# Spreading one more half of the attention weights by DMA, and loading the first weight matrix from two queues

## The chip, the cores and the metric

The kernel runs on one core of one Trainium2 chip. The metric is the device time of one execution in microseconds (us). PE is the TensorE matmul engine, PEld its weight loads, DVE the vector engine, ACT the scalar engine, POOL GpSimd, SP the engine that here only issues DMA. "The trace" is one profiled execution of a kernel; a kernel's timed set is 4 to 11 executions.

## The reference

One transformer block in bf16, 2048 positions of 1024 features: layer norm, a dilated local attention (32 heads, 8 keys for each query), the output projection, then a gated MLP whose gate mixes all positions. What matters here is the attention:

```python
qkv = (layernorm(x) @ wqkv)                 # wqkv: 1024 x 3072, wq is its first third
idx = pos[:, None] - 2 * arange(8)[None]    # 8 keys, two apart
logits = einsum('bhsd,bhswd->bhsw', q, k[idx]) * scale   # masked where idx < 0
attn = softmax(logits, axis=-1)
o = einsum('bhsw,bhswd->bhsd', attn, v[idx])
h = x + o @ wo                              # then the MLP block on layernorm(h)
```

## The kernel before

The positions are worked on in four chunks of 512. Before the main loop the kernel loads the first x tiles (128 positions each) and the weights wq in eight pieces of 256 KB, one for each group of 128 input features:

```python
dma(xts[0][0:64, :], x2d[0:64, :])            # dma = the SP queue
A.dma_start(xts[0][64:P, :], x2d[64:P, :])    # A.dma_start = the ACT queue
x_slot(1)
A.dma_start(xts[1], x2d[P:2 * P, :])
wsb = [wtile([P, KT, D], "wq", "wA"), ...]
for kt in range(KT):                          # KT = 8
    if kt == 6:
        load_x(2)
    dma(wsb[0][:, kt, :], wq_view[:, kt, 0:D])
load_x(3)
dma(wsb[1][:], wq_view[:, :, D:2 * D])        # wk, one DMA of 2 MB
```

Chunk 0's query projection consumes them at once. An x tile is normalized on DVE (`ln`), transposed on PE (`xpose`), and the transposes of tile i + 1 stand inside the matmuls of tile i, ahead of piece 5 (`QSPLIT = 5`):

```python
for i in range(TPC):                          # 4 tiles
    acc = new_acc()
    for kt in range(KT):
        if kt == 2 and i == 0:
            xpose(0, xns[0], (5, KT)); ln(1)
        if kt == QSPLIT and i + 1 < TPC:
            xpose(i + 1, xns[i + 1], (0, 4), (4, KT))
        for nh in range(2):
            T.matmul(acc[:, nh, :], xnT[0][:, kt, i * P:(i + 1) * P], wsb[0][:, kt, nh * CH:(nh + 1) * CH], ...)
    if i + 2 < TPC:
        ln(i + 2)
    ...
```

From then on all work is put into a static order for each engine by a small list scheduler in the kernel (`add(engine, cost, function, dependencies, ...)`).

After the softmax a weight exists once for each head and has to be spread over that head's 4 partitions before DVE can multiply it with v. For chunks 1 to 3 this is done by DMA (`ABDMA`): store the weights to DRAM from the ACT queue, load them back from the POOL queue with each row read four times. For chunk 0 it is done on PE, by matmuls with a 0/1 matrix `B4`, in two halves of four matmuls. Each matmul uses 32 of the 128 rows of the array, and the result is copied out of PSUM (the memory that matmuls write to) by ACT or DVE:

```python
ABDMA = (0, 1, 1, 1)
...
wait = add("DMA", BSLACK if hw else 0.0, lambda: None, [prev])
for sh in range(2):
    def pbm(sh=sh, ws=ws, hw=hw):
        if sh == 0:
            pb = ps_att.tile([P, 2, 4, P], FP32, name="pb", tag="L")      # one slot
        else:
            pb = ps_acc.tile([P, 2, 4, P], FP32, name="pba", tag="acc")
        for j in range(2):
            sq = 2 * sh + j
            T.matmul(pb[:, j], B4[32 * sq:32 * sq + 32, :], st["attn"][32 * sq:32 * sq + 32, ws, :],
                     start=True, stop=True, tile_position=(32 * sq, 0))
    ...
    eng = "DVE" if (hw == 0 and sh == 1) else "ACT"
    # a copy of pb into AB[:, hw, ...] on that engine
```

## Time and profile before

| | before |
|---|---|
| time, median of 4 | 725.91 us (725.59 to 726.45) |
| span of the profiled run | 723.9 us |
| PE busy | 718.5 us, 99% |
| DVE, ACT busy | 57%, 33% |
| matmuls | 3458 |

Two lines of the page: busy time of each engine with its share of the span and its count of instructions, and the chain of waits by engine.

```profile
PE 718.5 (99%) x3458; PEld 364.4 (50%) x3458; DVE 413.0 (57%) x435; ACT 240.0 (33%) x304; POOL 48.6 (7%) x56
...
PE 98%; DMA 1%; ACTq 0%; DVE 0%; SPq 0%; issue 0%
```

The second line is the chain of waits: followed back from the last instruction, 98% of the span is PE behind PE. Only PE work that goes away, idle time of PE that closes, or a new wait of PE can change the time. The idle time is all at the start. The timeline of PE (start, length, engine, line, what, how many; in brackets an idle stretch just before and what ended it):

```profile
7.45 1.04 PE L308 MATMUL acc<-wq,xnT 128*128 128x512 bf16 x4 [0.16 <-ACT xnT L269]
8.33 0.33 PE L267 MATMUL tpa<-csb,xn 128*128 128x128 bf16 x3
8.50 1.67 PE L308 MATMUL acc<-wq,xnT 128*128 128x512 bf16 x6
10.28 0.62 PE L267 MATMUL tpa<-csb,xn 128*128 128x128 bf16 x8
10.74 0.59 PE L308 MATMUL acc<-wq,xnT 128*128 128x512 bf16 x2
11.58 3.44 PE L308 MATMUL acc<-wq,xnT 128*128 128x512 bf16 x14 [0.25 <-DMA wq<-in_A_wqkv_dram]
14.86 0.61 PE L267 MATMUL tpa<-csb,xn 128*128 128x128 bf16 x8
```

L308 is the query projection, L267 the transposes of an x tile: tile 1's at 10.28, tile 2's at 14.86. Matmuls in a row cost 0.216 us each, so ten of them (2.16 us) with three small transposes should not need the 2.83 us from 7.45 to 10.28. There are holes here, and more up to 12.27, where wq piece 7 comes. From tile 2's transposes on, PE is dense.

Here is the broadcast on PE, in the same timeline. L553 are the broadcast matmuls, L396 ordinary projections:

```profile
67.21 1.05 PE L491 MATMUL L<-part,csb 128*32 128x512 bf16 x16
68.19 7.99 PE L396 MATMUL acc<-xnT,wk 128*128 128x512 bf16 x36
76.11 0.39 PE L553 MATMUL pb<-attn,csb 32*128 32x512 bf16 x2
76.12 0.39 PE L553 MATMUL pba<-attn,csb 32*128 32x512 bf16 x2
76.44 1.09 PE L396 MATMUL acc<-xnT,wk 128*128 128x512 bf16 x4
77.46 0.39 PE L553 MATMUL pba<-attn,csb 32*128 32x512 bf16 x2
77.61 0.39 PE L553 MATMUL pb<-attn,csb 32*128 32x512 bf16 x2
77.93 3.67 PE L396 MATMUL acc<-xnT,wk 128*128 128x512 bf16 x16
81.44 1.89 PE L396 MATMUL acc<-xnT,wv 128*128 128x512 bf16 x8
```

There are two breaks into the projection, one for each half.

### The profile page before, as it was taken

How to read it: one execution, taken by the hardware profiler on the slowest of the kernel's cores; microseconds unless marked ns; L12 is line 12 of the kernel's file. 1: busy time of each engine (PE TensorE's matmuls, PEld its weight loads, DVE VectorE, ACT ScalarE, POOL GpSimd, SP SyncE). 2: the span in 40 equal slices, each digit the busy share in tenths (PEclk: the TensorE clock that was granted, in tenths of full speed). 3: DMA queues.
4: the chain of work that ended last, by engine and by line, in shares of the span. 5: the costliest groups of instructions: out<-in, count | busy, mean ns of one | idle time of the engine just before them, and what ended most of it. 6: DMA issues, size and time to landing. Idle time of an engine off the chain costs nothing.

```text
span 723.9 us, 8455 instructions
## 1 busy us (share of the span) xinstructions
PE 718.5 (99%) x3458; PEld 364.4 (50%) x3458; DVE 413.0 (57%) x435; ACT 240.0 (33%) x304; POOL 48.6 (7%) x56
## 2 busy tenths in 40 slices
PE   8999999999999999999999999999999999999998
PEld 3666665666644444445445444444444444444444
DVE  5698999989998999876970202222222222222222
ACT  4389552633346785776735520000000000000000
POOL 0011200111002102000113000000000000000000
PEclk9999999999999999999999999999999999999999
DMA  8996464567664832642339979453116311120001
GB/s 303 278 299 134 145 175 148 159 213 254 211 255 147 230 149 75 229 138 71 140 113 261 251 196 293 158 139 120 33 43 138 119 35 44 39 87 7 1 22 66
DMA packets 119166, 107.09 MB, mean 148 GB/s; under 512 B 72568, under 2 KB 97304, under 8 KB 119128
## 3 DMA queue, kind: packets, MB, share of 16 engines
q1 hardware_dynamic: 110496, 73.88, 35.1%
q0 software_dynamic: 7616, 31.50, 12.7%
q10 hardware_dynamic: 1016, 1.18, 0.5%
q8 instruction: 27, 0.44, 0.3%
q14 instruction: 11, 0.09, 0.0%
HBM read 58.24 MB, written 31.52 MB: 124 GB/s over the span
## 4 chain that ended last, share of the span: by engine, by line
PE 98%; DMA 1%; ACTq 0%; DVE 0%; SPq 0%; issue 0%
PE acc L869 27%; PE acc L396 21%; PE acc L762 13%; PE acc L712 13%; PE acc L891 13%; PE acc L647 8%; PE acc L308 2%; DMA xp<-in_A_x_dram 1%; DMA wq<-in_A_wqkv_dram 1%; PE L L491 1%; PE tpa L267 0%; ACTq L227 0%; PE pb L553 0%; DVE ot L893 0%; SPq L234 0%; PE pba L553 0%
## 5 line engine op out<-in xcount | busy, mean ns | idle before, releaser
L452 DVE TENSOR_TENSOR prod<-qT,kT 128x4096 bf16<-128x4096 bf16 (+1 forms) x36 | 73.1, 2049 | 3.4 <-ACT kT L402 3.4
L712 PEld LDWEIGHTS <-hnT 128*128 128x128 bf16 x512 | 50.1, 98 | 47.2
L891 PEld LDWEIGHTS <-zg 128*128 128x128 bf16 x462 | 45.2, 98 | 51.8
L590 DVE TENSOR_TENSOR prod<-vT,AB 128x4096 bf16<-128x4096 bf16 (+1 forms) x31 | 64.2, 2083 | 0.8
L592 DVE TENSOR_TENSOR oT<-oT,prod 128x4096 bf16<-128x4096 bf16 (+1 forms) x31 | 64.4, 2079 | 0.1
L893 DVE TENSOR_TENSOR ot<-acc,hr 128x1024 bf16<-128x1024 f32 (+2 forms) x18 | 19.9, 1106 | 73.1 <-PE acc L891 73.1
L891 PE MATMUL acc<-wout_a,zg 128*128 128x512 bf16 (+1 forms) x264 | 58.2, 373 | 0.0
L712 PE MATMUL acc<-win_1467,hnT 128*128 128x512 bf16 x256 | 58.0, 379 | 0.0
L396 PE MATMUL acc<-xnT,wk 128*128 128x512 bf16 x256 | 56.7, 380 | 0.0
L762 PE MATMUL acc<-hnT,win_1667 128*128 128x512 bf16 x256 | 56.2, 379 | 0.0
L396 PE MATMUL acc<-xnT,wv 128*128 128x512 bf16 x256 | 55.9, 379 | 0.0
L647 PE MATMUL acc<-wo_sb,oT 128*128 128x512 bf16 x256 | 55.9, 379 | 0.0
L407 ACT CAST stg<-acc 128x1024 bf16<-128x1024 f32 x36 | 36.4, 1010 | 55.6 <-PE acc L396 48.3
L396 PEld LDWEIGHTS <-wk 128*128 128x128 bf16 x256 | 36.7, 145 | 18.8 <-issue 0.9
L396 PEld LDWEIGHTS <-wv 128*128 128x128 bf16 x256 | 37.0, 145 | 18.2
L891 PE MATMUL acc<-wout_b,zg 128*128 128x512 bf16 (+1 forms) x198 | 44.4, 373 | 0.0
L712 PE MATMUL acc<-win_1562,hnT 128*128 128x512 bf16 (+1 forms) x256 | 44.2, 326 | 0.0
L762 PE MATMUL acc<-hnT,win_1673 128*128 128x512 bf16 x192 | 42.4, 379 | 0.0
L396 PE MATMUL acc<-xnT,wq 128*128 128x512 bf16 x192 | 42.1, 379 | 0.0
L719 ACT ACTIVATE u<-acc 128x1024 bf16<-128x1024 f32 (+1 forms) x32 | 29.4, 918 | 35.1 <-PE acc L712 35.1
L647 PEld LDWEIGHTS <-oT 128*128 128x128 bf16 x256 | 25.1, 98 | 30.1
L762 PEld LDWEIGHTS <-win_1667 128*128 128x128 bf16 x256 | 25.0, 98 | 29.9 <-issue 0.4
(271 smaller groups left out, 955.1 us busy)
## 6 DMA issues: line engine op xcount, KB each, us to landing
z_d<-z1s SPq DMA_DIRECT2D x28, 256.0 KB, 2.6
z1c<-z_d SPq DMA_DIRECT2D x28, 256.0 KB, 2.7
z_d<-u SPq DMA_DIRECT2D x12, 448.0 KB, 2.5
xr<-in_A_x_dram SPq DMA_DIRECT2D x16, 256.0 KB, 2.9
h_d<-hb SPq DMA_DIRECT2D x16, 256.0 KB, 2.0
hr<-h_d SPq DMA_DIRECT2D x16, 256.0 KB, 3.2
out_dram<-ot SPq DMA_DIRECT2D x15, 256.0 KB, 2.0
xp<-in_A_x_dram SPq DMA_DIRECT2D x14, 256.0 KB, 5.6
```

The costliest lines, as they stand in the source:

```text
L396: G["mmins", c, xi, dp] = T.matmul(G[key][:, j, :], wv[:, kt, dl, :], xnT[c][:, kt, :], start=(kt == 0), stop=(kt == KT - 1))
L407: A.copy(stg[:], G[key][:])
L452: V.tensor_tensor(qs[w]["prod"][:, d0:d1], qT[:, d0:d1], kT[:, d0:d1, o:o + CH], op=ALU.mult)
L590: V.tensor_tensor(dst[:, :, sq].rearrange("p d (q s) -> p d q s", q=nq), vv, abb, op=ALU.mult)
L592: V.tensor_tensor(oTs[c][:, :, sq], oTs[c][:, :, sq], pvs[w, q0][:, :, sq], op=ALU.add)
L647: T.matmul(st["acc", il][:, nh, :], oTs[c][:, dl, il * P:(il + 1) * P], wo_sb[:, dl, nh * CH:(nh + 1) * CH], start=(dl == 0), stop=(dl == ...
L712: T.matmul(accf[:, n0:n1], hnTs[c][:, il, kt, :], wins[hf][:, kt, n0:n1], start=(kt == 0), stop=(kt == KT - 1))
L719: A.activation(st["u", il][:, hf * 1024:hf * 1024 + wd], G["accz", c, il, hf][:].rearrange("p a b -> p (a b)")[:, 0:wd], ACTF.Gelu_apprx_t ...
L762: T.matmul(G["accy", c, fp][:, j, :].rearrange("p (a b) -> p a b", a=TPC), wt[:, kt, f0 * P:(f0 + 1) * P], hnTs[c][:, :, kt, :], start=(kt ...
L869: m_ = T.matmul(acc[:, j, :], z2sb[a][:, f * P:(f + 1) * P], wspT[:, a, :], start=(a == 0), stop=(a == NT - 1))
L891: T.matmul(acc[:, m0 - n0:m1 - n0], zg[:, f, il * P:(il + 1) * P], wt[:, f0, m0:m1], start=(f == 0), stop=(f == NF - 1))
L893: V.tensor_tensor(ot[:, n0:n1], acc[:, 0:n1 - n0], hr[:, n0:n1], op=ALU.add)
```

## The change

The intent: take the second half of chunk 0's broadcast off PE (its consumer comes late enough for the DMA's latency), and get wq into the core sooner by loading pieces from both queues, with the x tiles that are needed later behind them.

```diff
-BSLACK = 1.0
-ABDMA = (0, 1, 1, 1)
+ABDMA = ((1,), (0, 1), (0, 1), (0, 1))
@@
-    A.dma_start(xts[1], x2d[P:2 * P, :])
     wsb = [wtile([P, KT, D], "wq", "wA"), wtile([P, KT, D], "wk", "wA"), wtile([P, KT, D], "wv", "wB")]
-    for kt in range(KT):
-        if kt == 6:
-            load_x(2)
-        dma(wsb[0][:, kt, :], wq_view[:, kt, 0:D])
+    for q, kt in ((dma, 0), (A.dma_start, 1), (dma, 2), (A.dma_start, None), (dma, 4), (A.dma_start, 3), (dma, 5), (dma, 6), (dma, 7)):
+        if kt is None:
+            q(xts[1], x2d[P:2 * P, :])
+        else:
+            q(wsb[0][:, kt, :], wq_view[:, kt, 0:D])
+    load_x(2)
     load_x(3)
@@ attention(c), for each half hw
-            if ABDMA[c]:
+            if by_dma:                       # by_dma = hw in ABDMA[c]
+                def keep(...):  A.dma_start(attn_d[c][hw]..., st["attn"][:, ws, :]...)
+                def spread(...): dma_w(st["AB"][:, hw]..., attn_d[c][hw]....to_broadcast([H, 4, 2048]))
+                kept = add("ACT", 0.35, keep, [prev], prio=0.0)
+                abs_[hw, 0] = abs_[hw, 1] = add("DMA", 6.5, spread, [kept], take=None if hw else "part")
                 continue
-            wait = add("DMA", BSLACK if hw else 0.0, lambda: None, [prev])
  ... (the matmul branch stays for the first half; the old all-or-nothing DMA branch goes)
```

More of the change, by code (lines that the diff above doesn't have):

```diff
@@ L531, in attention, with new_ab, at, keep @@
         prev = add("DVE", 0.92, rec, [prev], prio=3.0)
-        abs_, ats = {}, []
+        abs_ = {}
+        def new_ab():
+            st["AB"] = att.tile([P, 2, TPC, W_WIN // 2, P], BF16, name="AB", tag="part", bufs=2)
         for hw in range(2):
             ws = slice(4 * hw, 4 * hw + 4)
-            def at(ws=ws, hw=hw):
-                if hw == 0 and not ABDMA[c]:
-                    st["AB"] = att.tile([P, 2, TPC, W_WIN // 2, P], BF16, name="AB", tag="part", bufs=2)
+            by_dma = hw in ABDMA[c]
+            def at(ws=ws, alloc=not hw and not by_dma):
+                if alloc:
+                    new_ab()
                 V.tensor_tensor(st["attn"][:, ws, :], st["sme"][:, 1, ws, :], st["rinv"][:].unsqueeze(1).to_broadcast([P, 4, P]), op=ALU.mult)
-            prev = add("DVE", 0.61, at, [prev], prio=3.0, lat=0.1, take="part" if hw == 0 and not ABDMA[c] else None, free="prod" if hw else None)
-            ats.append(prev)
-            if ABDMA[c]:
+            prev = add("DVE", 0.61, at, [prev], prio=3.0, lat=0.1, take=None if hw or by_dma else "part", free="prod" if hw else None)
+            if by_dma:
+                def keep(hw=hw, ws=ws):
+                    A.dma_start(attn_d[c][hw].rearrange("h q w s -> q h (w s)"), st["attn"][:, ws, :].rearrange("p w s -> p (w s)"))
+                def spread(hw=hw):
+                    if hw == 0:
+                        new_ab()
+                    dma_w(st["AB"][:, hw].rearrange("p q w s -> p (q w s)"),
+                          attn_d[c][hw].rearrange("h q w s -> h (q w s)").unsqueeze(1).to_broadcast([H, 4, 2048]))
+                kept = add("ACT", 0.35, keep, [prev], prio=0.0)
+                abs_[hw, 0] = abs_[hw, 1] = add("DMA", 6.5, spread, [kept], take=None if hw else "part")
                 continue
-            wait = add("DMA", BSLACK if hw else 0.0, lambda: None, [prev])
             for sh in range(2):
@@ L554, in pbm, with cp @@
                                  start=True, stop=True, tile_position=(32 * sq, 0))
-                pm = add("PE", 0.2, pbm, [wait], prio=1.0, take="acc" if sh else "L", lat=0.2)
-                eng = "DVE" if (hw == 0 and sh == 1) else "ACT"
-                def cp(sh=sh, ws=ws, hw=hw, eng=eng):
-                    (V.tensor_copy if eng == "DVE" else A.copy)(
-                        st["AB"][:, hw, 2 * sh:2 * sh + 2], st["pb", hw, sh][:])
-                abs_[hw, sh] = add(eng, 1.25 if eng == "DVE" else 0.91, cp, [pm], prio=1.0 if eng == "ACT" else 2.9,
-                                   free="acc" if sh else "L", lat=0.15)
-        if ABDMA[c]:
-            for k in range(2):
-                def keep(k=k):
-                    A.dma_start(attn_d[c][k].rearrange("h q w s -> q h (w s)"), st["attn"][:, 4 * k:4 * k + 4, :].rearrange("p w s -> p (w s)"))
-                def spread(k=k):
-                    if k == 0:
-                        st["AB"] = att.tile([P, 2, TPC, W_WIN // 2, P], BF16, name="AB", tag="part", bufs=2)
-                    dma_w(st["AB"][:, k].rearrange("p q w s -> p (q w s)"),
-                          attn_d[c][k].rearrange("h q w s -> h (q w s)").unsqueeze(1).to_broadcast([H, 4, 2048]))
-                kept = add("ACT", 0.35, keep, [ats[k]], prio=0.0)
-                abs_[k, 0] = abs_[k, 1] = dma_op(6.5, spread, [kept])
-            abs_[0, 0].take = ("part",)
+                pm = add("PE", 0.2, pbm, [prev], prio=1.0, take="acc" if sh else "L", lat=0.2)
+                eng = "DVE" if sh else "ACT"
+                def cp(sh=sh, hw=hw, eng=eng):
+                    (V.tensor_copy if eng == "DVE" else A.copy)(st["AB"][:, hw, 2 * sh:2 * sh + 2], st["pb", hw, sh][:])
+                abs_[hw, sh] = add(eng, 1.25 if sh else 0.91, cp, [pm], prio=2.9 if sh else 1.0, free="acc" if sh else "L", lat=0.15)
         G["at", c] = prev
```

## The prediction

> **What bounds the kernel now.** PE. The page has PE busy 718.5 of 723.9 us, and the chain of waits is 98% PE: after 12.27 us every step of it up to 720.5 us is a matmul behind a matmul, granted clock 1.00 throughout. So only two things can move the time: PE work that goes away, and the bubbles before 12.27 us. DVE (57%) and ACT (33%) are off the chain.
>
> **Spread of chunk 0's second half.** Removed: four of the eight broadcast matmuls (32x512), two copies of ACT (1.02 us each) out of PSUM, one accumulator slot. Added: one store of the weights (issue on ACT about 0.5 to 1.1 us) and one broadcast load of 512 KB from POOL, as chunks 1 to 3 already do. In the chain the stretch 76.18 to 78.00 us holds the eight broadcast matmuls and four ordinary ones; ordinary ones cost 0.216 us in the chain (64 in 13.81 us), so the eight cost 1.82 - 0.86 = 0.96 us and four about 0.48 us. All of that is on PE, so all of it is gained: -0.48 us. The new path: weights ready 75.4, store about 3 us, load 4.7 us median to landing: about 84.5 us. The timeline's first multiply that needs it (window step 4) starts at 92.2; the output projection that waits for the last of these starts at 114.4 and DVE is done at 110.3. So nothing there should wait; ACT's relief (about 1.5 us) is worth nothing.
>
> **Start.** PE lost between 7.45 and 12.27 us, in the fine timeline: 0.35 us for wq piece 4, 0.3 for x tile 1's normalized tile (10.28), 0.4 for piece 6 (11.58), 0.25 for piece 7 (12.27). The DMA view says that engines are busy 0.9 to 1.05 from 4 to 11 us and pieces land 0.68 us apart: it is bandwidth, not issue. The Trainium skill, "DMA: Bandwidth & Descriptors", section "Issuing engines are not separate DMA queues", says that several issuing engines share the same 16 DMA engines and save issue time only; this trace agrees (300 GB/s while both queues carry data, 390 to 410 afterwards with one).
> So a second queue gives no bandwidth. It changes order: x tiles 2 and 3 move behind wq. The last wq piece should land about 0.65 us earlier (256 KB less before it, near 11.6 us), but x tile 2 lands near 12.2 in place of 10.88, and x tile 1, now behind a wq piece on its queue, near 8.2 in place of 7.56. From landing to a normalized tile takes 2.7 us: tile 1's transposes near 10.9 (10.28 before), tile 2's near 14.9 (14.86 before). Bubbles for wq turn into bubbles for x; from there PE is dense. Start: about 0, between -0.6 and +0.8 us.
>
> **Prediction.** 725.87 - 0.48 - 0.1: 725.3 us, range 724.5 to 726.2. Faster by over 2%: 0.01; within 2%: 0.98; slower: 0.01.
>
> **What would show it.** PE matmuls 3454 instead of 3458; only one pair of copies out of the broadcast's PSUM tiles; the chain near 76 us shorter by 0.5 us; the spread's load landing before 90 us with no DVE wait on it. At the start: piece 7 no longer last to be waited for; DVE's wait for x tile 2 longer; tile 2's transposes within 0.6 us of 14.86. After that the chain again all PE.
>
> **What would make it wrong.** The ACT queue getting less than half of the packets, so that x tile 1 or wq piece 3 lands past 9.5 us (+1 us or more); a faster ramp of two queues, which would give up to -0.7; ACT's table load pushed behind its DMA issues past 5.6 us; the list order of the later work changing so that PE waits somewhere, which nothing in the trace prepares.

## The result

| | before | after |
|---|---|---|
| time, median of 4 | 725.91 us (725.59 to 726.45) | 725.23 us (724.50 to 725.79) |
| span of the profiled run | 723.9 us | 723.8 us |
| first query matmul | 7.45 us | 7.16 us |
| transposes of x tile 1 | 10.28 us | 11.52 us |
| transposes of x tile 2 | 14.86 us | 15.43 us |
| last addition of DVE | 720.55 us | 720.50 us |
| from tile 2's transposes to that addition ("the body") | 705.69 us | 705.07 us |

The ratio is 0.9989, with a 95% interval from 0.9972 to 1.0007: the same within the noise of the set. The measured 725.23 lies 0.07 from the predicted 725.3.

The table's last rows split the profiled run in two. The body became 0.62 us shorter, the start 0.57 us longer, and in this pair of traces the sum is about nothing (the timed medians differ by 0.68 us). The same two lines of the page after:

```profile
PE 714.0 (99%) x3392; PEld 364.1 (50%) x3454; DVE 413.0 (57%) x435; ACT 238.2 (33%) x302; POOL 49.6 (7%) x57
...
PE 98%; DMA 1%; issue 0%; DVE 0%; ACTq 0%; ACT 0%
```

PE's count is not a fall of 66: 62 matmul records are missing from this trace, and the weight loads, one for each matmul, give 3454, four fewer than before. ACT has two copies fewer. PE's start, where the two waits are now piece 3 of wq (9.86) and tile 1's normalized x (11.52):

```profile
7.16 1.04 PE L308 MATMUL acc<-wq,xnT 128*128 128x512 bf16 x4
8.03 0.33 PE L267 MATMUL tpa<-csb,xn 128*128 128x128 bf16 x3
8.20 0.59 PE L308 MATMUL acc<-wq,xnT 128*128 128x512 bf16 x2
9.86 1.02 PE L308 MATMUL acc<-wq,xnT 128*128 128x512 bf16 x4 [1.07 <-DMA wq<-in_A_wqkv_dram]
11.52 0.62 PE L267 MATMUL tpa<-csb,xn 128*128 128x128 bf16 x8 [0.63 <-DVE xn L255]
11.97 3.62 PE L308 MATMUL acc<-wq,xnT 128*128 128x512 bf16 x15
15.43 0.61 PE L267 MATMUL tpa<-csb,xn 128*128 128x128 bf16 x8
```

Behind 11.52 PE is dense: 11.97 + 16 x 0.216 = 15.43, so tile 2, which now comes last, was not waited for. DVE's timeline shows when the tiles came (L243 is the first instruction on an x tile). Here are tile 1 and tile 2, before:

```profile
7.59 0.69 DVE L243 BATCH_NORM_STATS2 bnst<-xp 128x6 f32<-128x512 bf16 x1 [0.52 <-DMA xp<-in_A_x_dram]
...
10.90 0.69 DVE L243 BATCH_NORM_STATS2 bnst<-xp 128x6 f32<-128x512 bf16 x1 [0.68 <-DMA xp<-in_A_x_dram]
```

and after:

```profile
8.82 0.69 DVE L243 BATCH_NORM_STATS2 bnst<-xp 128x6 f32<-128x512 bf16 x1 [1.90 <-DMA xp<-in_A_x_dram]
...
12.18 0.69 DVE L243 BATCH_NORM_STATS2 bnst<-xp 128x6 f32<-128x512 bf16 x1 [0.71 <-DMA xp<-in_A_x_dram]
```

Tile 1 is 1.23 us later, behind piece 1 on the ACT queue. That it comes later repeats in the experiments below, the size does not: DVE began on tile 1 at 8.08 to 8.82 us in the four traces with the split queues (after, e2, e4, e11), and at 6.80 to 7.96 in the seven with the old start. The broadcast after, with one break instead of two:

```profile
67.78 1.05 PE L491 MATMUL L<-part,csb 128*32 128x512 bf16 x16
68.76 7.13 PE L396 MATMUL acc<-xnT,wk 128*128 128x512 bf16 x31
75.83 0.39 PE L563 MATMUL pb<-attn,csb 32*128 32x512 bf16 x2
75.83 0.39 PE L563 MATMUL pba<-attn,csb 32*128 32x512 bf16 x2
76.15 5.40 PE L396 MATMUL acc<-xnT,wk 128*128 128x512 bf16 x24
81.39 1.89 PE L396 MATMUL acc<-xnT,wv 128*128 128x512 bf16 x8
```

(One of the 32 ordinary matmuls of the second line has lost its record.) From L491 to the first matmul of wv it takes 13.61 us, 14.23 before: the 0.62 us of the body are all here. The new path is not waited for: POOL issues the load at 79.93, it lands at 83.61, and DVE's first multiply with that half starts at 92.39, straight behind its previous work.

### The profile page after: what moved, and what is told of

It is laid out like the page before. It is cut to its first block, busy times and chain, and to the rows that moved or that the text cites. A ratio compares the mean times of both kernels' runs of the same rounds, so it can differ in the third digit from the quotient of the medians.

```text
span 723.8 us, 8387 instructions
## 1 busy us (share of the span) xinstructions
PE 714.0 (99%) x3392; PEld 364.1 (50%) x3454; DVE 413.0 (57%) x435; ACT 238.2 (33%) x302; POOL 49.6 (7%) x57
## 4 chain that ended last, share of the span: by engine, by line
PE 98%; DMA 1%; issue 0%; DVE 0%; ACTq 0%; ACT 0%
PE acc L865 27%; PE acc L396 21%; PE acc L758 13%; PE acc L887 13%; PE acc L708 13%; PE acc L643 8%; PE acc L308 2%; DMA xp<-in_A_x_dram 1%; PE L L491 1%; PE tpa L267 0%; ACTq L233 0%; DVE bnst L243 0%; ACTq L226 0%; DVE bnst L244 0%; DVE xn L255 0%
```

## The experiments

There were twelve runs in three sets (e1 to e4, e5 to e8, e9 to e12); the kernels of a set ran on one chip with the kernel before beside them. Three runs repeat a kernel: e8 the one before, e11 the changed one, e12 that of e1. The working theory was that there are two independent parts: the body gains PE time, and the start loses some of it to a later tile 1. The rivals were that the spread's gain is something other than PE time, and that in the timed runs the start is the gain.

The measure that the experiments turn on is the table below: tile 2's transposes (what the start cost) and the body. "GB/s" is what the DMA engines moved from 4.5 to 7.5 us.

| run | spread | start | tile 1 | tile 2 | body | GB/s | time, median (range) | before, same chip |
|---|---|---|---|---|---|---|---|---|
| before | no | old | 10.28 | 14.86 | 705.69 | 309 | 725.91 (725.59 to 726.45) | |
| after | half | new | 11.52 | 15.43 | 705.07 | 316 | 725.23 (724.50 to 725.79) | 725.91 |
| e1 | half | old | 9.87 | 14.42 | 705.07 | 380 | 724.51 (724.21 to 724.73) | 725.28 |
| e2 | no | new | 11.03 | 15.09 | 705.71 | 332 | 725.89 (725.14 to 727.00) | 725.28 |
| e3 | no | order only | 10.40 | 15.10 | 705.70 | 295 | 725.67 (725.36 to 727.23) | 725.28 |
| e4 | no | queues only | 11.21 | 15.12 | 705.69 | 340 | 725.90 (725.29 to 726.86) | 725.28 |
| e5 | half, matmuls kept | old | 10.66 | 15.35 | 706.02 | 265 | 725.88 (725.19 to 726.39) | 725.79 |
| e6 | both halves | old | 10.02 | 14.37 | 706.78 | 342 | 726.34 (726.09 to 727.56) | 725.79 |
| e7 | no | one queue | 9.87 | 14.31 | 705.70 | 348 | 725.19 (724.84 to 726.27) | 725.79 |
| e8 | no | old | 10.01 | 14.85 | 705.69 | 342 | 725.38 (724.91 to 727.28) | 725.79 |
| e9 | half, matmuls kept together | old | 9.99 | 14.13 | 705.55 | 374 | 724.90 (724.72 to 725.23) | 725.35 |
| e10 | half | one queue | 10.19 | 14.29 | 705.07 | 354 | 724.70 (724.39 to 725.07) | 725.35 |
| e11 | half | new | 10.78 | 14.70 | 705.08 | 394 | 724.83 (724.65 to 725.35) | 725.35 |
| e12 | half | old | 9.86 | 14.49 | 705.07 | 355 | 724.47 (724.32 to 724.64) | 725.35 |

One run of the kernel before in the set of e5 to e8 took 946.48 us at a clock of 0.753; it is left out of everything.

### e1_spread_only: the spread without the new start

```diff
 (the changed kernel, with the loads at the start put back as they were)
```

> The kernel before with only the second half of chunk 0's spread by DMA; the loads at the start as before. Theory (the two parts add; the spread takes 0.6 us of PE work away, the new start gives about as much back in the profiled run): 0.5 to 0.7 us under the kernel before, 725.3 or less, tile 2's transposes at 14.9 us as before, and the value projection of chunk 1 (first matmul at 81.44 before) near 80.8. Rival (the gain of the change is the start in unprofiled runs, the spread is worth nothing because PE's work is refilled or waits move): equal to before within 0.2 us.

Measured: 724.51 us, ratio 0.9985 (0.9973 to 0.9998), body 705.07 us, the first matmul of wv at 80.39. The body is the changed kernel's to the hundredth. The theory holds for the body. The rest of the 0.77 us is put down to the start, which in this trace was 0.44 us shorter than in the trace of before although the loads are the same; see e8.

### e2_start_only: the new start without the spread

```diff
 (the kernel before, with the changed kernel's loop over q, kt and load_x(2), load_x(3) behind it)
```

> The kernel before with only the new loads at the start. Theory: 0.0 to 0.6 us slower than before; x tile 1 lands near 8.8 us, its transposes start near 11.5, tile 2's near 15.4, and all that follows is shifted by the same 0.57 us. Rival (the start is the gain): 0.3 us or more faster than before in the timed runs.

Measured: 725.89 us against 725.28, ratio 1.0007 (0.9994 to 1.0019). Body 705.71, so nothing but the start moved. Tile 1's transposes came at 11.03 and tile 2's at 15.09, both earlier than I expected from the trace of after. The rival, a gain of 0.3 us or more, is not seen; the medians say a loss of 0.61 us, but the interval includes 1, so it is not clear of noise.

### e3_order_only and e4_queues_only: the two parts of the new start

e3, against the kernel before:

```diff
     for kt in range(KT):
-        if kt == 6:
-            load_x(2)
         dma(wsb[0][:, kt, :], wq_view[:, kt, 0:D])
+    load_x(2)
     load_x(3)
```

e4, against the new start (e2):

```diff
     for q, kt in (...):
+        if kt == 6:
+            load_x(2)
         ...
-    load_x(2)
     load_x(3)
```

> The kernel before with x tiles 2 and 3 behind all pieces of wq, but all pieces from the one queue as before and x tile 1 first on the other queue. Theory (what costs time in the new start is the second queue, which delays x tile 1 and piece 3, not the order): x tile 1's transposes stay near 10.3 us, piece 7 lands near 11.6, tile 2 lands near 12.2, its transposes start within 0.2 us of 14.9: time within 0.2 us of before. Rival (the order costs): tile 2's transposes near 15.4 and 0.5 us slower.

> The kernel before with wq pieces 1 and 3 moved to the other queue with x tile 1 between them, and x tile 2 still ahead of pieces 6 and 7. Theory (the second queue costs): x tile 1's transposes near 11.5 us as in the changed kernel, tile 2's at 15.4 or later (pieces 6 and 7 land 0.7 us later than in the changed kernel, near 12.2): 0.5 to 0.8 us slower than before. Rival (the order costs, the queues are free): tile 2's transposes near 14.9 and time as before.

Measured: 725.67 and 725.90 us, both not separable from before (725.28; intervals 0.9993 to 1.0018 and 0.9993 to 1.0020). The traces tell more than the times. In these traces each part alone brings tile 2's transposes to 15.1, by another road. In e3 tile 1 is on time (10.40) and PE then waits for tile 2's normalized x, as the timeline of e3 shows:

```profile
10.40 0.62 PE L266 MATMUL tpa<-csb,xn 128*128 128x128 bf16 x8
...
15.10 0.62 PE L266 MATMUL tpa<-csb,xn 128*128 128x128 bf16 x8 [0.62 <-DVE xn L254]
```

In e4 PE waits for piece 3 and for tile 1, and is dense from there:

```profile
9.67 1.02 PE L310 MATMUL acc<-wq,xnT 128*128 128x512 bf16 x4 [0.90 <-DMA wq<-in_A_wqkv_dram]
11.21 0.62 PE L269 MATMUL tpa<-csb,xn 128*128 128x128 bf16 x8 [0.52 <-DVE xn L257]
...
15.12 0.61 PE L269 MATMUL tpa<-csb,xn 128*128 128x128 bf16 x8
```

So my theory (only the second queue can cost time) was wrong: the order makes a wait of its own. In the traces of after, e2, e3 and e11, where tile 2 is loaded behind all of wq, DVE began on it at 11.94 to 12.33 us, against 10.17 to 11.43 with the old start; with the 2.7 us from there to PE it cannot be transposed before some 14.6 to 15.1. That the order costs as much as the queues is not shown: it is one trace each, and with the old start tile 2's transposes scatter from 14.13 to 15.35 (see e8). With both parts (e2, 15.09) the delays don't add, because PE runs late from tile 1 on and tile 2 is there in time.

### e5_mm_back and e9_mm_back_joined: the broadcast matmuls put back, without use

```diff
 e5, in the DMA branch of chunk 0's second half
+                if c == 0:
+                    for sh in range(2):
+                        (the two matmuls of pbm(sh) into a PSUM tile that nobody reads)
+                        add("PE", 0.2, idle_pbm, [prev], prio=1.0, take=..., free=..., lat=0.2)
 e9: the same four matmuls in one add("PE", 0.4, ...)
```

> The spread alone (old start), but the four broadcast matmuls of the second half are still done on PE, into accumulators that nobody reads (the result stays right; two ACT copies fewer, as in the change). Theory (the spread gains PE's time for four matmuls and nothing else): from tile 2's transposes at the start to the last addition of DVE 705.7 us as in the kernel before (705.07 with the spread), so equal to before within 0.2 us plus the scatter of the start. Rival (the gain comes from the copies and accumulators that ACT and DVE no longer hold): 705.1 us, 0.6 us faster than before.

> As e5, but the four idle broadcast matmuls stand together in PE's order (in e5 they stood as two pairs, each breaking into the projection, and 706.02 us from tile 2's transposes to the last addition came out, 0.95 over the spread alone). Theory (each break into the projection has a cost of its own beside the matmuls, about 0.15 us, and PE's time is all that the spread gains): 705.7 us within 0.1, as in the kernel before. Rival (the matmuls are nearly free and something else cost 0.95): 705.1 us, or 706.0 as in e5.

Both give the right result. The body is 706.02 in e5 and 705.55 in e9, against 705.07 with the spread alone and 705.69 before. So e5 missed what I had expected by 0.33 us and e9 by 0.14 (0.1 had been allowed), in opposite directions. The matmuls do account for PE's time, but not by the piece. In e5 the scheduler put the two pairs into two places, as its timeline shows, and they cost 0.95 us, 0.475 for each pair:

```profile
77.09 0.39 PE L561 MATMUL pba<-attn,csb 32*128 32x512 bf16 x2
...
79.29 0.39 PE L561 MATMUL pb<-attn,csb 32*128 32x512 bf16 x2
```

In e9 the four stand together and cost 0.48 in all. Here is the timeline of e9, whose second break (L561) is the one put back:

```profile
74.85 2.81 PE L395 MATMUL acc<-xnT,wk 128*128 128x512 bf16 x12
77.60 0.39 PE L561 MATMUL pb<-attn,csb 32*128 32x512 bf16 x2
77.61 0.39 PE L561 MATMUL pba<-attn,csb 32*128 32x512 bf16 x2
77.93 2.81 PE L395 MATMUL acc<-xnT,wk 128*128 128x512 bf16 x12
```

What costs is the break: 0.48 us for each, with two matmuls in it or with four. That fits the Trainium skill, "TensorEngine Tiling (Array Packing)", section "Tiling Modes", Key Properties: tiles of the array run in parallel, and a change of the tiling mode drains the array. The pairs start 0.00 to 0.01 us apart here, so the first half of the statement is seen; that what the 0.48 us hold beyond one matmul's 0.216 is such a drain is the page's explanation, not shown by a run.

In the kernel before, the second break cost 0.14 us more (0.62). A kernel with no break at all confirms the sum: from the 16 matmuls of L490 (L491 in the other two) to the first matmul of wv, e6 takes 13.13 us, the changed kernel 13.61 and the kernel before 14.23, so the breaks cost 0.48 and 0.62. In the second, the two pairs start at 77.46 and 77.61. The second pair needs the one PSUM slot "L", which ACT empties from 76.54 to 77.55. It starts 0.06 us after that. So some 0.14 us of the gain may be an accumulator that was not free. This is read from the times; no run has isolated it.

### e6_spread_all: the first half by DMA too

```diff
-ABDMA = ((1,), (0, 1), (0, 1), (0, 1))
+ABDMA = ((0, 1), (0, 1), (0, 1), (0, 1))     (with the old start)
```

> Old start, both halves of chunk 0 spread by DMA, no broadcast matmul left. Theory (PE is never idle behind the weights in this stretch as long as its order has other work): another 0.5 to 0.6 us less than with one half, 704.5 us from tile 2's transposes to the last addition. Rival (the first half's weights come about 6 us later by DMA, DVE stands idle for them near 77 to 84 us, and the output projection at 114.4, which has 4.1 us of slack, comes late or a later wait appears on PE): PE waits at the output projection or later, and the time is equal to or over that of one half.

Measured: 726.34 us against 725.79, ratio 1.0009 (0.9997 to 1.0021), the highest median of all but not clear of noise; the body, 706.78, is. The saving that the theory promised is there, 0.48 us, as the stretch without a break shows (66.72 to 79.85 is 13.13 us, against 13.61 with one break):

```profile
66.72 1.05 PE L490 MATMUL L<-part,csb 128*32 128x512 bf16 x16
67.70 12.31 PE L395 MATMUL acc<-xnT,wk 128*128 128x512 bf16 x56
79.85 3.40 PE L395 MATMUL acc<-xnT,wv 128*128 128x512 bf16 x15
```

But the rival holds: more is lost later. DVE stands idle before its first multiply:

```profile
83.06 2.29 DVE L585 TENSOR_TENSOR oT<-vT,AB 128x4096 bf16<-128x4096 bf16 x1 [6.03 <-DMA AB<-attn_d]
```

The output projection goes from 113.19 (e1) to 117.05 us, and PE fills that time with other matmuls. The bill comes 200 us later, where DVE and ACT have to deliver the MLP's normalized input:

```profile
318.81 1.04 PE L707 MATMUL acc<-win,hnT 128*128 128x512 bf16 x4 [1.59 <-DMA hnT<-hb]
```

The body is 1.71 us longer than e1's although 0.48 are saved, so 2.19 us are lost behind the broadcast. This one wait is 1.59 of them; the rest has not been traced.

### e7_one_queue, e8_before_again and e10_one_queue_spread: is it the second queue, and how much does the start scatter?

```diff
-    A.dma_start(xts[1], x2d[P:2 * P, :])
     for kt in range(KT):
+        if kt == 2:
+            dma(xts[1], x2d[P:2 * P, :])
         if kt == 6:
             load_x(2)
 (e7 on the kernel before, e10 with the spread; e8 is the kernel before, unchanged)
```

> The kernel before, with x tile 1 moved from the second queue into the first, between wq pieces 1 and 2; x tile 2 ahead of pieces 6 and 7 as before. Theory (two queues in use at once carry 300 GB/s, one carries 390): the packets' rate from 4.5 to 7.5 us is 370 GB/s or more, everything lands up to 0.8 us earlier, tile 2's transposes at or before 14.2 us: 0.3 to 0.7 us faster. Rival (the low rate before 7.5 us belongs to the time, not to the number of queues): rate 300 to 330 GB/s in 4.5 to 7.5 us and tile 2's transposes within 0.4 us of 14.9.

> The kernel before, unchanged, for the scatter of the start: the same loads in the run with the spread alone had tile 2's transposes at 14.42 us, in the run of before at 14.86. Theory (the start's DMA timing scatters by some tenths of a us from run to run, the rest does not): tile 2's transposes between 14.3 and 15.0 us, 705.7 us from there to the last addition within 0.05 us. Rival (the spread itself shortened the start): 14.86 within 0.1 us.

> The spread of the second half together with x tile 1 in the first queue between pieces 1 and 2 (e7's start). If the parts add: 705.07 us from tile 2's transposes to the last addition, transposes near 14.3 to 14.4 us in the median, 724.4 us, 0.2 to 0.4 under the spread alone with the old start, whose start scatters around 14.75 (worked out from the times of 34 runs). Rival (the start of e7 is only a lucky draw of the same scatter): the same time as the spread alone.

Measured: e7 725.19 us against 725.79 (0.9993; 0.9981 to 1.0005), tile 2's transposes at 14.31. e8 725.38, at 14.85. e10 724.70, at 14.29, not better than the spread alone on the same chip (724.47, e12). The theory behind e7, that one queue carries more, falls: its rate was 348 GB/s, and the old start with its two queues has had 265 to 380 in seven traces. The start of e7 is fast in both traces, yet e10's time shows no gain, so the rival of e10 is not refuted.

The seven traces with the old start (before, e1, e5, e6, e8, e9, e12) have the same instructions up to tile 2, and tile 2's transposes at 14.13 to 15.35 us. The body, in contrast, repeats within 0.02 us for each program. In the trace that starts latest (e5), the rate was the lowest, 265 GB/s. The timed sets scatter too: the kernel before alone has taken 724.87 to 727.73 us in 38 fast runs. How much of that is the start is not shown, since only one execution of each run was traced. e8 by itself would not tell the two readings of its expectation apart, since its 14.85 us is that of before again; e5 does, which has the spread and starts latest of all, so the spread doesn't shorten the start.

### e11_after_again and e12_spread_again: the changed kernel and the spread alone side by side

```diff
 (no edit: the changed kernel; and e1's kernel)
```

> The changed kernel, unchanged, once more, beside the spread alone on the same chip. Theory: 705.07 us from tile 2's transposes on, transposes at 14.4 to 16 us, median of the times 0.2 to 0.6 us over the spread alone's. Rival (the new start is as good as the old one): equal medians.

> The spread alone once more, beside the changed kernel. Theory: 705.07 us from tile 2's transposes on; times 0.5 to 0.9 us under the kernel before, and 0.2 to 0.6 under the changed kernel. Rival: equal to the changed kernel.

Measured: 724.83 us (724.65 to 725.35) and 724.47 us (724.32 to 724.64), five runs each. The ranges don't touch, though only just (by 0.01 us). The new start costs 0.36 us in the medians here. The traces are less clear: tile 2's transposes came at 15.43, 15.09 and 14.70 us with the new start (after, e2, e11), where the old one has 14.13 to 15.35: the two overlap nearly whole. What repeats is the cause of the wait: in all three PE waits for tile 1's normalized x (by 0.63, 0.29 and 0.45 us) and is dense from there to tile 2. Against the kernel before on the same chip (725.35) the two are at ratios of 0.9996 (0.9983 to 1.0008) and 0.9990 (0.9977 to 1.0002).

e11 also settled a reading of mine. The windows view of e11 from 4.5 to 7.5 us gives the length, busy time and count of PE, PEld, DVE, ACT and POOL, the granted clock, the DMA share and, last, the GB/s:

```profile
4.50:7.50 3.00, 1.95 (x10) 0.63 (x8) 2.43 (x7) 0.69 (x3) 0.00 (x0) 1.00 1.05 394
```

In the DMA view of the same window, these are its two hardware queues (q1 is SP's, q10 ACT's; packets, MB, share of the 16 engines' time):

```profile
q1 hardware_dynamic: 328, 0.60, 54.4%
q10 hardware_dynamic: 313, 0.58, 50.0%
```

Two queues in equal use carried 394 GB/s, more than one queue in e7. The windows view of the kernel before, where one queue was nearly alone in the second window:

```profile
4.50:7.50 3.00, 2.78 (x11) 0.93 (x10) 2.13 (x7) 0.77 (x3) 0.00 (x0) 1.00 0.94 309
7.50:10.50 3.00, 2.83 (x17) 1.24 (x18) 2.21 (x5) 1.06 (x3) 0.00 (x0) 1.00 1.06 402
```

## Why the prediction was right or wrong

The time was right, 725.23 measured against 725.3. Point by point:

1. **PE bounds, and only PE work or the start can move the time.** Right. The body is the same within 0.02 us in every program that has the same PE work (705.69 to 705.71 in six traces, 705.07 to 705.08 in five), whatever the start did. e6 adds the limit: when more work is taken off PE, a wait for another engine can come up and cost more than was gained.
2. **The spread gains 0.48 us.** Right in kind, too small: 0.62. The term "four matmuls, about 0.48 us" was mis-sized. Two things were off in it. The stretch in which it was counted (76.18 to 78.00) starts behind the gap that the first break makes: the 36 matmuls before it take 7.92 us, where 36 x 0.216 is 7.78. So the eight cost 1.10 us (14.23 against 13.13 in e6) and not 0.96. And the two halves are not alike: the first break costs 0.48 (as in e9), the second, which was taken away, 0.62. The cost is also not one of matmuls, as I had counted it: two alone cost 0.475 (e5).
3. **ACT's relief is worth nothing; the new load is early enough.** ACT's two copies stay out in e9 too, and e9's body is still 0.48 us longer than the spread's, so most of the gain does not come from them. The remaining 0.14 us may (the slot "L" is emptied by an ACT copy), so "nothing" is not shown. The load landed at 83.61, predicted 84.5; needed at 92.39.
4. **A second queue gives no bandwidth.** Right. I cited the Trainium skill, "DMA: Bandwidth & Descriptors", section "Issuing engines are not separate DMA queues", for it, and the traces agree: from 7.5 to 10.5 us the changed kernel moved 399 GB/s, the kernel before 402. But the evidence that I put beside it, 300 GB/s with two queues and 390 to 410 with one, was a coincidence of time, as e11 shows (394 with two).
5. **The order changes: piece 7 near 11.6, tile 2 near 12.2, tile 1 near 8.2.** In the trace piece 7 landed at 11.49 and DVE began on tile 2 at 12.18, as predicted. It began on tile 1 at 8.82. Tile 1 was third on its queue, behind half of tile 0 and a wq piece; I had worked with an even share of the packets; by the DMA view of the changed kernel that queue, ACT's, had 98 packets to SP's 207 from 1 to 4.5 us, and 263 to 248 from 4.5 to 7.5. Tile 1's transposes came at 11.52 (10.9 predicted).
6. **"Bubbles for wq turn into bubbles for x; tile 2's near 14.9."** Half right, and this is the step that failed in the changed kernel. Tile 2 does not bind there; piece 3 and tile 1 do, and PE is late by them before tile 2 matters. e3 shows that the wait I had named is real when it stands alone (0.62 us for tile 2's normalized x). The start was to cost 0.1 us. The profiled run has 0.57; against the spread alone on one chip the medians say 0.36 (e11, e12); against the kernel before, e2 says 0.6, with an interval that includes no cost at all.
7. **What would show it.** 3454 matmuls (by their weight loads), one pair of copies, no wait for the load, the chain all PE: as predicted. Piece 7 is no longer the last piece waited for, as predicted; piece 3 is. Tile 2's transposes within 0.6 us of 14.86: true by 0.03. DVE's wait for tile 2 longer: by 0.03 us only, 0.71 against 0.68; the wait for tile 1 grew, from 0.52 to 1.90. The warning that piece 3 might land past 9.5 us came true (PE takes it up at 9.86). An uneven share is not the whole reason: in e2 the ACT queue had 453 of the two queues' 863 packets from 1 to 7.5 us, and piece 3 was still taken up only at 9.71, as the fourth load on that queue.
8. **The sum.** My two errors had opposite signs: 0.14 us too little gain, and too small a loss at the start. With a scatter of 1.2 us at the start (14.13 to 15.35), hitting within 0.07 us is luck; the range was wide enough for both errors.

What stays open is the exact cost of the new start (0.0 to 0.6 us by these sets), and what makes the rate of the first loads differ from run to run.

The version that the experiments point to is the spread with the old start (e1, e12): 0.77 and 0.88 us under the kernel before by the medians on the same chips, 0.36 under the changed kernel. Of the 0.77 and 0.88, 0.62 are the body; the rest is put down to the start. The medians of e1 and e12 are the lowest of all that were tried, but no version is 2% from another, and e10's range (724.39 to 725.07) overlaps e12's.

## What to carry to other kernels

When one engine is busy 99% of the time, cut the trace at a point from which that engine is dense, and compare the two parts on their own: here a repeatable gain of 0.62 us and a scattering start of the same size hid each other in the profiled pair. Count a small job that interrupts a stream of matmuls by the break it makes, not by its matmuls; here two groups of two cost twice as much (0.95 us) as one group of four (0.48). Before more work is moved off that engine, ask which later wait it will bring up: in e6 another 0.48 us were saved and 2.19 lost. Here the first loads were limited by bandwidth (the DMA engines were busy 0.94 to 1.06 of the time from 4.5 to 10.5 us before and after), and another queue only changed who came later. In such a case, list the landing time and the first use of each piece before moving one.

## What the Trainium skill lacked or had wrong

- "TensorEngine Tiling (Array Packing)", section "Tiling Modes": it says that a change of mode drains the array, without a figure. Here a break of 32-row matmuls (512 columns) into a stream of 128-row ones cost 0.475 us with two matmuls (e5) and 0.48 with four (e9).
- "DMA: Bandwidth & Descriptors": it has no word on how far the rate of a program's first loads scatters. With the same loads it was 265 to 380 GB/s from 4.5 to 7.5 us in seven traces, and 393 to 404 from 7.5 to 10.5 us in the same seven.
- The same page, section "Queues, rings and completion order", says that each DMA engine takes packets from its queues in turn. The shares agree when both queues are full (54.4% and 50.0% of the engines' time in e11). It gives no figure for what this does to a transfer's landing: DVE began on the 256 KB of x tile 1 at 6.80 to 7.96 us as the second transfer on the ACT queue (seven traces with the old start) and at 8.08 to 8.82 as the third (after, e2, e4, e11).
